# A GLU's last weight: all low parts on VectorE, a ring of six for the plain products' tokens, the first pair in another place

## The chip, the cores and the metric

The kernel runs on one core of a Trainium2 chip. The metric is the device time of one execution in microseconds; the time of a kernel is the median of its runs. TensorE multiplies, VectorE and ScalarE prepare its operands and take its results away, GpSimd (POOL) helps with elementwise work and issues the scatters of the output, SyncE (SP) issues nearly all transfers. Each engine works through its own instructions in order, and so does SP's queue of transfers.

## What is computed

Attention with a bias that decays with position, then a mixture of experts, then a gated linear unit. The change lies in the last of these. Cut to that part, the reference is:

```
def _moe2_ref(x, w_gate, w_val, w_out):           # x: 2304 tokens of 512; w_gate, w_val: 512 x 1536; w_out: 1536 x 512
    gate = 1.0 / (1.0 + np.exp(-(x @ w_gate)))
    val = x @ w_val
    return (gate * val @ w_out).astype(np.float32)
```

All numbers are float32.

## The kernel before

TensorE takes each float32 operand as two parts: a high part, which ScalarE makes by a cast to fp32r, and a low part, which is the operand minus its high part and comes from an elementwise subtraction. A product is then three matmuls: high by high, high by low, low by high.

The gated unit is class Moe2. Its first half makes h = gate * val for three blocks of 768 tokens (t = 0, 1, 2) and writes them to DRAM (`hd[t]`, shown as h). It runs as units (f, t, m) of seven slots; the last unit is n - 1, and two pieces of it, slot(n, 2) and slot(n, 4), run among the products that follow. The second half multiplies h by the last weight, w_out, and this is where the change lies. It has two stages.

**The plain products** (block 0). `final(q)`, q = 0 to 23, q = 12 g + f: for 384 tokens (group g) it adds the product of the f-th 128 rows of h with part f of the weight, nine matmuls of 512 columns (L1482 in the profile). It needs three things:

- part f of the weight, high and low. `load_o` brings twelve parts of 128 x 512 into four tiles `wr` (places a0_0 to a0_3 of the pool keep); `o_high(f)` casts on ScalarE (L1411), `o_low(f)` subtracts (L1417), on VectorE for f = 0 and 2, on GpSimd for the other ten.
- h of this f and g. `load_h(q)` (L1454) brings it into one of four tiles, the ring a1_4, a1_5, a1_0, a1_1. Load q + 4 stands in SP's queue behind `final(q)` and goes when that product has read the tile. `h_tasks(q)` then makes the high part on ScalarE (L1459) and the low part on VectorE (L1460); these stand two products ahead of `final(q)`.
- a PSUM accumulator for each of three rows of tokens. After f = 11 three copies (L1488, two on ScalarE and one on VectorE) and three scatters (L1464, GpSimd) take it away.

**The pair stage** (blocks 1 and 2). Six pairs j of 2 x 128 tokens each go through seven products by Strassen's scheme in Winograd's form (`p_slot(j, s)`, L1534). It needs sums of the weight's parts: `o_sums` makes eight sums in place in `wr` on VectorE (L1424) and from each of the four `wr` tiles a high part (`to`, ScalarE, L1439) and a low part (`to`, L1441: tiles 0 and 2 on VectorE, 1 and 3 on GpSimd). And it needs h of the pair: `load_p(j)` brings it in four transfers (tiles hp, L1501), and `p_tasks(j)` makes seven forms of it: casts on ScalarE (hf, L1261), low parts and sums on VectorE (hf, L1262, and hp, L1263). Before, `load_p(0)` goes into a1_2 and a1_6, and the loads of the other pairs take turns between a0_0 with a0_1 and a0_2 with a0_3, where `wr` was.

All this small work is placed by hand: a table `todo` says after which slot of the units a task is written, a table `later` after which product (its key is q). An engine sees its instructions in the order in which they are written. So what stands ahead of what on VectorE, ScalarE and SP follows from these tables, and within one key from the order of the `put` calls.

Of the kernel before, what the change touches and what calls it, by code (L numbers as in the profile page):

```python
# [8 lines left out]
F32 = mybir.dt.float32  # L9
F32R = mybir.dt.float32r  # L10
# [5 lines left out]
ALU = mybir.AluOpType  # L16
# [1185 lines left out]
class Moe2:  # L1202
# [210 lines left out]
        return high  # L1413

    def o_low(self, f):
        eng = self.nc.vector if f in (0, 2) else self.nc.gpsimd
        return lambda: eng.tensor_tensor(self.po[f][1], self.scr[f], self.po[f][0].bitcast(F32), ALU.subtract)  # L1417

    def o_sums(self):

        nc = self.nc
        W = [self.wr[i] for i in range(4)]
        lo, hi = slice(0, 256), slice(256, 512)
        sub = lambda o, x, y: lambda: nc.vector.tensor_tensor(o, x, y, ALU.subtract)  # L1424
        S = []
        for k in range(2):
            u, v = W[k], W[2 + k]
            S += [
                sub(u[:, :, lo], u[:, :, hi], u[:, :, lo]), sub(u[:, :, hi], v[:, :, hi], u[:, :, hi]),
                sub(v[:, :, hi], v[:, :, hi], u[:, :, lo]), sub(v[:, :, lo], v[:, :, lo], v[:, :, hi]),  # L1430
            ]
        self.to = {}

        def high(i, h):
            def f():
                tag = f"a2_{2 * i + h}" if 2 * i + h < 7 else "sg2"
                self.to[i, h] = self.ap.tile([128, 3, 512], F32R, tag=tag, name="to", bufs=1)
                if h == 0:
                    nc.scalar.copy(self.to[i, 0], W[i])  # L1439
                else:  # L1440
                    (nc.gpsimd if i % 2 else nc.vector).tensor_tensor(self.to[i, 1], W[i], self.to[i, 0].bitcast(F32), ALU.subtract)  # L1441

            return f

        return S, [high(i, h) for i in range(4) for h in range(2)]

    RING = (4, 5, 0, 1)

    def load_h(self, q):
        g, f = divmod(q, 12)
        t = self.hl[q] = self.ap.tile([128, 3, 512], F32R, tag=f"a1_{self.RING[q % 4]}", name="h0", bufs=1)[:, :, : self.G]
        self.nc.sync.dma_start(t[:, 2].bitcast(F32), self.hd[0][:, f, self.G * g : self.G * g + self.G])  # L1454

    def h_tasks(self, q):
# [36 lines left out]
    def load_p(self, j):  # L1493
        t, c0 = 1 + j // 3, 256 * (j % 3)
        raws = []
        for i in range(2):
            p, tag = (self.ap, f"a1_{(2, 6)[i]}") if j == 0 else (self.keep, f"a0_{2 * (j % 2) + i}")
            w = p.tile([128, 2, 6, 128], F32, tag=tag, name="hp", bufs=1)
            raws += [w[:, 0], w[:, 1]]
        for d, (i, h) in zip(raws, ((0, 0), (1, 1), (0, 1), (1, 0))):  # L1500
            self.nc.sync.dma_start(d, self.hd[t][:, 6 * h : 6 * h + 6, c0 + 128 * i : c0 + 128 * i + 128])  # L1501
        self.hr[j] = raws
# [86 lines left out]
    def run(self, ctx, rest):  # L1589

        NF, NT = self.NF, self.NT
        P = lambda c, n, **kw: c.enter_context(self.tc.tile_pool(name=n, bufs=1, reuse_waits="tile", **kw))
        self.ps, self.ap = P(ctx, "o_ps", space=PSUM), P(ctx, "o_a")
        self.units = [
            (f, t, m) for f in range(NF)
            for t, m in ([(0, 0), (0, 1), (1, 0), (2, 0), (1, 1), (2, 1)] if f == 0 else [(t, m) for m in range(2) for t in range(NT)])
        ]
        n = len(self.units)
        todo, self.late = {}, []

        def put(at, tasks):
            todo.setdefault(at, []).extend(tasks)

        def spread(first, last, tasks):
            for i, task in enumerate(tasks):
                put(first + (last - first + 1) * i // len(tasks), [task])

        at = lambda u, s: 7 * u + s
        for i, tasks in enumerate(rest):
            put(at(0, i), tasks)  # L1610
        raws = [[], [self.ap.tile([128, 2, self.G], F32, name=f"xs{i}", bufs=1) for i in range(3)]]
        raws[1].append(self.rp.tile([128, 1024], F32, tag="raw2_3", name="xs3", bufs=1)[:, : 2 * self.G].rearrange("p (c t) -> p c t", c=2))
        for i in range(2):
            w = self.ap.tile([128, 2, 2, self.G], F32, tag=f"a2_{5 + i}", name="xs", bufs=1)
            raws[0] += [w[:, 0], w[:, 1]]
        self.room_x(1, self.ap)
        for t in range(1, NT):
            self.load_x(t, raws[t - 1])
        spread(at(1, 0), at(2, 2), self.x_tasks(1, raws[0]))
        put(at(2, 2), [lambda: self.room_x(2, self.ap)])  # L1620
        spread(at(2, 3), at(3, 4), self.x_tasks(2, raws[1]))
        put(at(5, 0), [self.rows()])
        free = 0
        for f in range(1, NF):
            b = 6 * f - 6
            for m, soon, there in ((0, at(b + 1, 5), at(b + (4 if f == 1 else 3), 5)), (1, at(b + 4, 5), at(b + 6, 5))):
                soon = max(soon, free)
                blocks, parts = self.w_tasks(m)
                for stages, k in zip(blocks, (0, 1, 7, 8)):
                    for i, task in enumerate(stages):  # L1630
                        put(soon + k + i, [task])
                there = max(there, soon + 12)
                for i, tasks in enumerate(parts):
                    put(there + i, tasks)
                free = there + len(parts)
        put(at(n - 2, 5), [lambda: self.load_o(0)])
        put(at(n - 1, 0), [lambda: [(self.load_h(q), self.load_h(q + 1), self.load_o(1 + q // 2)) for q in (0, 2)]])
        put(at(n - 1, 1), [lambda: self.load_o(3)])
        oh, ol = [self.o_high(f) for f in range(12)], [self.o_low(f) for f in range(12)]
        for f in range(4):  # L1640
            put(at(n - 1, f + 1), [oh[f]])
            put(at(n - 1, f + 2), [ol[f]])
        for q in range(2):
            put(at(n - 1, 5 + q), self.h_tasks(q))
        for u in range(n):
            for s in range(7):
                now, self.late = self.late, []
                self.slot(u, s)
                for task in todo.pop(7 * u + s, []) + now:
                    task()  # L1650
        assert not todo
        later = {}

        def put(at, tasks):
            later.setdefault(at, []).extend(tasks)

        put(0, [lambda: self.slot(n, 2)])
        put(1, [lambda: self.slot(n, 4), lambda: [store() for store in self.late]])
        for q in range(2, 24):
            put(q - 2, self.h_tasks(q))  # L1660
        for f in range(4, 12):
            put((f - 4) // 2, [oh[f], ol[f]])
        sums, parts = [], []
        put(5, [lambda: [x.extend(y) for x, y in zip((sums, parts), self.o_sums())]])
        for i in range(8):
            put(6 + i, [lambda i=i: sums[i]()])
            put((10, 11, 14, 15, 11, 12, 15, 16)[i], [lambda i=i: parts[i]()])
        put(9, [lambda: self.load_p(0)])
        put(17, [lambda: self.load_p(1)])
        p = []  # L1670
        put(15, [lambda: p.extend(self.p_tasks(0))])
        cuts = (0, 2, 4, 6, 8, 11, 13, 15)
        for k in range(7):
            put(16 + k, [lambda i=i: p[i]() for i in range(cuts[k], cuts[k + 1])])
        for q in range(24):
            self.final(q)
            if q + 4 < 24:
                self.load_h(q + 4)
            for task in later.pop(q, []):
                task()  # L1680
        assert not later
        for j in range(self.NP + 1):
            for s in range(7):
                self.p_slot(j, s)
                if (j, s) == (0, 0):
                    for task in p[15:]:
                        task()
                if j + 1 < self.NP:
                    if s == 0:
                        x = self.p_tasks(j + 1)  # L1690
                    for task in x[(0, 0, 2, 5, 8, 11, 13)[s] : (0, 2, 5, 8, 11, 13, 18)[s]]:
                        task()
                if s == 6 and j + 2 < self.NP:
                    self.load_p(j + 2)
# [156 lines left out]
```

## Time and profile before

| | |
|---|---|
| runs shown | 988.88, 988.88, 997.13 us; median 988.88 |
| the profiled execution | 993.5 us, its span 991.7 us |
| TensorE busy over the span | 932.6 us (94%) |
| VectorE busy | 714.6 us (72%) |
| ScalarE busy | 557.3 us (56%) |
| GpSimd busy | 434.9 us (44%) |
| mean granted clock of TensorE | 0.981 of full speed |

Times of the trace are microseconds from the start of the span. Matmuls are pipelined: the duration shown for one includes its way through the array, so the rate is read from starts, or from a long unbroken piece of the chain of waits. PE is TensorE, DVE is VectorE, ACT is ScalarE, POOL is GpSimd, SP is SyncE; a q behind the name (SPq) means the engine's queue. In brackets behind an instruction stands the idle time before it and what ended it. The granted clock is given as a share of full speed; it has two levels, 1.2 and 2.4 GHz, so a mean between 0.5 and 1 is a mixture.

### The profile page before, as it was taken

Reading aid. Unit: us, or ns where it says so; the run is one execution under the profiler, and the core shown is the slowest. Engines: PE = TensorE matmul, PEld = TensorE weight load, DVE = VectorE, ACT = ScalarE, POOL = GpSimd, SP = SyncE. Lnnn points to the kernel's source line nnn. Section 1 sums busy time; section 2 is a strip of 40 time slices with the busy share of each in tenths; the row PEclk is TensorE's granted clock in tenths of the full one; section 3 lists DMA queues with packets and bytes.
Section 4 is the critical chain, followed back from the end, with each engine's and each line's share of the span. In section 5 each row is a group of like instructions: output and inputs, shape, how many; then the busy total and the mean of one; then the engine's idle time right before and its main releaser. Section 6 shows DMA issues by size and latency. Waiting matters only on the chain. (4 is left out here: it accounts for less than half of the span.)

```text
span 991.7 us, 18860 instructions
## 1 busy us (share of the span) xinstructions
PE 932.6 (94%) x6261; PEld 863.9 (87%) x6261; DVE 714.6 (72%) x1573; ACT 557.3 (56%) x1328; POOL 434.9 (44%) x639
## 2 busy tenths in 40 slices
PE   7999999999887999999999779999999999879996
PEld 6887888777676999999998769999999998659996
DVE  6889989998865678867635686776575747667771
ACT  5988888887623556666633454544445344434431
POOL 7877787896863577876540000100000006222111
PEclk8999999999998999999999989999999999999999
DMA  6655448794674145922357522332332307553411
GB/s 165 156 128 137 111 91 96 175 111 71 213 67 59 59 150 160 329 87 86 117 164 262 150 67 85 96 107 95 108 122 84 113 25 265 181 167 106 148 57 43
DMA packets 164578, 124.32 MB, mean 125 GB/s; under 512 B 86897, under 2 KB 146828, under 8 KB 164470
## 3 DMA queue, kind: packets, MB, share of 16 engines
q1 hardware_dynamic: 159462, 112.57, 43.6%
q0 software_dynamic: 3792, 10.14, 3.1%
q8 instruction: 52, 0.85, 0.4%
q14 instruction: 56, 0.46, 0.2%
q10 hardware_dynamic: 1216, 0.30, 0.1%
HBM read 115.95 MB, written 32.18 MB: 149 GB/s over the span
## 5 line engine op out<-in xcount | busy, mean ns | idle before, releaser
L1326 PE MATMUL X<-a,set 128*128 128x384 f32 x864 | 166.6, 341 | 7.6 <-ACT u L1335 4.3
L1326 PEld LDWEIGHTS X<-a,set 128*128 128x128 f32 x864 | 154.1, 192 | 9.6 <-ACT u L1335 4.9
L845 POOL TENSOR_SCALAR dn<-dr 128x256 int8<-128x256 int8 (+1 forms) x60 | 33.7, 562 | 262.6 <-DMA dr<-in_moe_w_gate_dram 118.1
L170 POOL TENSOR_SCALAR bias<-cumB,cumT 128x576 f32<-128x576 f32 (+4 forms) x155 | 82.5, 534 | 41.8 <-DVE nm L289 30.9
L909 POOL TENSOR_TENSOR w<-raw,w 128x512 fp32r<-128x512 f32 x56 | 79.3, 1427 | 41.4 <-ACT w L906 38.5
L973 PE MATMUL ph<-xT,w 128*128 128x256 f32 x672 | 92.0, 287 | 1.9 <-DVE w L909 1.9
L298 ACT ACTIVATE P<-P,nm 64x64 f32<-64x64 f32 (+4 forms) x160 | 89.6, 563 | 2.7 <-DVE nm L289 2.6
L973 PEld LDWEIGHTS ph<-xT,w 128*128 128x128 f32 x672 | 85.4, 194 | 2.1 <-DVE w L909 2.1
L289 DVE CUSTOM_DVE_ANT_0 P<-sb,bias 128x576 f32<-128x576 f32 (+4 forms) x160 | 72.0, 479 | 17.9 <-PE sb L280 14.6
L1326 PE MATMUL Y<-a,set 128*128 128x384 f32 x432 | 81.1, 335 | 0.0
L339 DVE TENSOR_TENSOR PL<-pt,PH 128x512 fp32r<-128x512 f32 (+3 forms) x160 | 78.8, 530 | 2.7 <-ACT PH L331 1.7
L1326 PEld LDWEIGHTS Y<-a,set 128*128 128x128 f32 x432 | 75.8, 188 | 0.1
L331 ACT CAST PH<-pt 128x512 fp32r<-128x512 f32 (+3 forms) x160 | 67.0, 466 | 9.8 <-PE pt L317 7.1
L317 PE MATMUL pt<-ident,P 128*128 128x128 f32 (+2 forms) x480 | 69.2, 274 | 1.4 <-DVE PL L339 0.8
L977 ACT ACTIVATE hH<-ph 128x256 fp32r<-128x256 f32 x72 | 27.7, 385 | 75.2 <-PE ph L973 65.3
L1464 POOL DMA_INDIRECT out_dram<-oy,row x18 | 20.9, 1163 | 108.0 <-ACT oy L1549 56.2
L909 DVE TENSOR_TENSOR w<-raw,w 128x512 fp32r<-128x512 f32 x56 | 59.9, 1071 | 11.1 <-ACT w L906 10.3
L1335 ACT COPY u<-X 128x384 f32<-128x384 f32 x72 | 34.5, 479 | 59.1 <-PE X L1326 59.0
L317 PEld LDWEIGHTS pt<-ident,P 128*128 128x128 f32 (+2 forms) x480 | 52.6, 130 | 13.1 <-issue 6.6
L906 ACT CAST w<-raw 128x512 fp32r<-128x512 f32 x112 | 63.5, 619 | 0.0
L362 PE MATMUL ot<-PH,vhl 128*128 128x512 f32 (+4 forms) x160 | 62.0, 398 | 0.0
L280 PE MATMUL sb<-KT,QH 128*128 128x288 f32 (+3 forms) x192 | 56.2, 317 | 4.1 <-DVE nm L289 3.3
(299 smaller groups left out, 2424.5 us busy)
## 6 DMA issues: line engine op xcount, KB each, us to landing
raw<-in_moe_w_dram SPq DMA_DIRECT2D x80, 512.0 KB
h<-sg SPq DMA_DIRECT2D x72, 192.0 KB
cumB<-cum_d SPq DMA_DIRECT2D x32, 288.0 KB
hp<-h SPq DMA_DIRECT2D x24, 384.0 KB
qraw<-in_q_dram SPq DMA_DIRECT2D x58, 128.0 KB
dr<-in_moe_w_out_dram SPq DMA_DIRECT2D x12, 511.6 KB
dr<-in_moe_w_gate_dram SPq DMA_DIRECT2D x24, 255.2 KB
dr<-in_moe_w_val_dram SPq DMA_DIRECT2D x24, 255.2 KB
```

Source lines behind the costliest of these rows:

```text
L170: (nc.vector if n in FILLB else nc.gpsimd).tensor_scalar(res[i][:rows], cumB[:rows, :m], -1.0, self.cumT[:rows, i, n : n + 1], ALU.mult, A ...
L280: nc.tensor.matmul(self.sb[:rows, o : o + c1 - c0], X[:, T0[i] : T0[i] + rows], h["KT"][:, c0:c1], start=j == 0, stop=j == 1)
L289: nc.vector.tensor_tensor_reduce(out=pt[:rows], in0=self.sb[:rows, o : o + m], in1=self.bias_t[n][i][:rows], op0=ALU.add, op1=ALU.min, sca ...
L298: nc.scalar.activation(h["P"][i][:rows], h["P"][i][:rows], AF.Exp, bias=h["nm", i][:rows], scale=-1.0, accum_out=self.sums_t[(n // 2) % 3] ...
L317: nc.tensor.transpose(pt[: TS[j], c : c + TS[i]], h["P"][i][: TS[i], T0[j] : T0[j] + TS[j]], self.ident[: TS[i], : TS[i]])
L331: nc.scalar.copy(t[:r, a:z], pt[:r, a:z])
L339: nc.vector.tensor_tensor(t[:r, a:z], pt[:r, a:z], h["H"][u][:r, a:z].bitcast(F32), ALU.subtract)
L362: nc.tensor.matmul(out[:, q0 : q0 + z - a], w, X[: TS[j], a:z], start=k == 0, stop=k == len(mm) - 1, skip_group_check=True)
L906: nc.scalar.copy(v, src)
L909: (eng or nc.vector).tensor_tensor(v, src, h.bitcast(F32), ALU.subtract)
L973: nc.tensor.matmul(ph, w[:, 128 * dc : 128 * dc + 128], x[:, dc], start=k == 0, stop=k == 11)
L1326: self.nc.tensor.matmul(bank, w[:, c], a[:, h, c], start=first and k == 0, stop=k == 5, skip_group_check=True)
```

## The change

`o_low` subtracts all twelve parts on VectorE, and so does the low part of every `to`. The ring has six tiles, a1_4, a1_5, a1_0, a1_1, a1_2, a1_6, with loads 4 and 5 written among the slots of the last unit. Since a1_2 and a1_6 now belong to the ring, the first pair goes to a0_0 and a0_1, the place of the first two `wr` tiles, and the keys of the sums, the `to` parts, the pairs' loads and the first pair's tasks move.

```
     def o_low(self, f):
-        eng = self.nc.vector if f in (0, 2) else self.nc.gpsimd
-        return lambda: eng.tensor_tensor(self.po[f][1], self.scr[f], self.po[f][0].bitcast(F32), ALU.subtract)
+        return lambda: self.nc.vector.tensor_tensor(self.po[f][1], self.scr[f], self.po[f][0].bitcast(F32), ALU.subtract)
...
                 else:
-                    (nc.gpsimd if i % 2 else nc.vector).tensor_tensor(self.to[i, 1], W[i], self.to[i, 0].bitcast(F32), ALU.subtract)
+                    nc.vector.tensor_tensor(self.to[i, 1], W[i], self.to[i, 0].bitcast(F32), ALU.subtract)
...
-    RING = (4, 5, 0, 1)
+    RING = (4, 5, 0, 1, 2, 6)
...
-        t = self.hl[q] = self.ap.tile([128, 3, 512], F32R, tag=f"a1_{self.RING[q % 4]}", name="h0", bufs=1)[:, :, : self.G]
+        t = self.hl[q] = self.ap.tile([128, 3, 512], F32R, tag=f"a1_{self.RING[q % 6]}", name="h0", bufs=1)[:, :, : self.G]
...
-            p, tag = (self.ap, f"a1_{(2, 6)[i]}") if j == 0 else (self.keep, f"a0_{2 * (j % 2) + i}")
-            w = p.tile([128, 2, 6, 128], F32, tag=tag, name="hp", bufs=1)
+            w = self.keep.tile([128, 2, 6, 128], F32, tag=f"a0_{2 * (j % 2) + i}", name="hp", bufs=1)
...
+        for q in (4, 5):
+            put(at(n - 1, 2 * q - 5), [lambda q=q: self.load_h(q)])
...
-        put(5, [lambda: [x.extend(y) for x, y in zip((sums, parts), self.o_sums())]])
+        put(3, [lambda: [x.extend(y) for x, y in zip((sums, parts), self.o_sums())]])
         for i in range(8):
-            put(6 + i, [lambda i=i: sums[i]()])
-            put((10, 11, 14, 15, 11, 12, 15, 16)[i], [lambda i=i: parts[i]()])
-        put(9, [lambda: self.load_p(0)])
-        put(17, [lambda: self.load_p(1)])
+            put((4, 5, 6, 7, 8, 8, 9, 10)[i], [lambda i=i: sums[i]()])
+            put((8, 9, 11, 12, 9, 13, 12, 14)[i], [lambda i=i: parts[i]()])
+        put(12, [lambda: self.load_p(0)])
+        put(15, [lambda: self.load_p(1)])
         p = []
-        put(15, [lambda: p.extend(self.p_tasks(0))])
-        cuts = (0, 2, 4, 6, 8, 11, 13, 15)
+        put(13, [lambda: p.extend(self.p_tasks(0))])
+        cuts = (0, 2, 4, 6, 8, 9, 11, 13, 15, 18)
...
-            if q + 4 < 24:
-                self.load_h(q + 4)
+            if q + 6 < 24:
+                self.load_h(q + 6)
...
-                if (j, s) == (0, 0):
-                    for task in p[15:]:
-                        task()
```

What the change moves is seen in the order of instructions on three engines. Line numbers behind the edits fall by one to three (L1482 becomes L1481, L1460 becomes L1459, L1417 becomes L1416, L1441 becomes L1440). Numbers in names are tiles in the order in which they were made.

VectorE at the first products. h_14605, h_14607, h_14613 and h_14615 are h of products 0 to 3 and h_14703, h_14729 of products 4 and 5. Before, from the last low part that VectorE has:

```order
L1417 TENSOR_TENSOR set<-wr,set 128x512
L1460 TENSOR_TENSOR h_14605<-h_14605 128x384
L1354 TENSOR_TENSOR u_14685<-Y,u_14685 128x384
L1356 TENSOR_TENSOR sg<-u_14685,sg 128x384
L1460 TENSOR_TENSOR h_14607<-h_14607 128x384
L1356 TENSOR_TENSOR sg<-X,sg 128x384
L1460 TENSOR_TENSOR h_14613<-h_14613 128x384
L1354 TENSOR_TENSOR u_14652<-Y,u_14652 128x384
L1356 TENSOR_TENSOR sg<-u_14652,sg 128x384
L1460 TENSOR_TENSOR h_14615<-h_14615 128x384
L1460 TENSOR_TENSOR h_14703<-h_14703 128x384
L1460 TENSOR_TENSOR h_14729<-h_14729 128x384
```

and now, from the same place on, where h_14654 and h_14677 are h of products 4 and 5:

```order
L1459 TENSOR_TENSOR h_14613<-h_14613 128x384
L1416 TENSOR_TENSOR wo<-wr,wo 128x512 x2
L1354 TENSOR_TENSOR u_14652<-Y,u_14652 128x384
L1356 TENSOR_TENSOR sg<-u_14652,sg 128x384
L1459 TENSOR_TENSOR h_14615<-h_14615 128x384
L1416 TENSOR_TENSOR set<-wr,set 128x512 x2
L1459 TENSOR_TENSOR h_14654<-h_14654 128x384
L1416 TENSOR_TENSOR set<-wr,set 128x512 x2
L1459 TENSOR_TENSOR h_14677<-h_14677 128x384
L1416 TENSOR_TENSOR wo<-wr,wo 128x512 x2
```

Eight low parts of the weight now stand in pairs between h of products 2 and 6.

VectorE around the first pair's first low part (`hf`). h_14839, h_14853, h_14870, h_14888 and h_14917 are h of products 13 to 17. Now:

```order
L1487 COPY oy<-acc 128x512
L1459 TENSOR_TENSOR h_14839<-h_14839 128x384
L1459 TENSOR_TENSOR h_14853<-h_14853 128x384
L1440 TENSOR_TENSOR to<-wr,to 128x1536
L1459 TENSOR_TENSOR h_14870<-h_14870 128x384
L1440 TENSOR_TENSOR to<-wr,to 128x1536
L1459 TENSOR_TENSOR h_14888<-h_14888 128x384
L1440 TENSOR_TENSOR to<-wr,to 128x1536
L1262 TENSOR_TENSOR hf<-hp,hf 128x768
L1459 TENSOR_TENSOR h_14917<-h_14917 128x384
```

Before, two of these three `to` were GpSimd's, the sums of `wr` were spread over the same products, and `hf` stood behind h of product 18. Now three `to` and `hf` stand ahead of h of products 15, 16 and 17.

SP's queue around the pairs' loads. Before, h_14861 is the load of product 13 and h_15013 that of product 21:

```order
L1454 DMA h_14861<-h_65 128x384
L1501 DMA hp<-h_66 128x6x128 x4
L1454 DMA h_14881<-h_65 128x384
L1454 DMA h_14912<-h_65 128x384
L1454 DMA h_14933<-h_65 128x384
L1454 DMA h_14949<-h_65 128x384
L1454 DMA h_14963<-h_65 128x384
L1454 DMA h_14978<-h_65 128x384
L1454 DMA h_14995<-h_65 128x384
L1454 DMA h_15013<-h_65 128x384
L1501 DMA hp<-h_66 128x6x128 x4
L1454 DMA h_15036<-h_65 128x384
```

and now, where h_14935 is the load of product 18 and h_15014 that of product 22:

```order
L1453 DMA h_14935<-h_65 128x384
L1499 DMA hp<-h_66 128x6x128 x4
L1453 DMA h_14958<-h_65 128x384
L1453 DMA h_14973<-h_65 128x384
L1453 DMA h_14991<-h_65 128x384
L1499 DMA hp<-h_66 128x6x128 x4
L1453 DMA h_15014<-h_65 128x384
L1453 DMA h_15029<-h_65 128x384
```

The first pair's four transfers move from behind the load of product 13 to behind that of product 18, and the second pair's follow them three loads later.

## Rows read from the trace of the kernel before

**Rows 1.** Windows: length, busy PE, PEld, DVE, ACT, POOL (instructions), clock, DMA share, GB/s.

```profile
820.00:893.00 73.00, 63.33 (x274) 50.55 (x273) 53.28 (x59) 31.67 (x54) 27.14 (x16) 0.98 0.63 201
893.00:985.00 92.00, 90.59 (x755) 90.18 (x753) 58.57 (x76) 36.31 (x61) 15.41 (x15) 1.00 0.28 93
...
860.00:871.00 11.00, 5.87 (x23) 3.82 (x22) 8.84 (x8) 4.08 (x6) 4.13 (x2) 1.00 0.43 154
871.00:877.00 6.00, 6.00 (x20) 4.71 (x19) 4.98 (x5) 4.23 (x7) 3.49 (x1) 0.72 0.11 33
```

**Rows 2.** Groups by line, 820 to 895: count | busy, mean ns | idle before, releasers.

```profile
L1482 PE MATMUL acc<-set,h 128*128 128x512 f32 x126 | 30.5, 393 | 3.2 <-ACT h L1459 2.2 <-DVE h L1460 1.0
L1482 PE MATMUL acc<-wo,h 128*128 128x512 f32 x90 | 24.7, 423 | 6.4 <-DVE h L1460 3.5 <-ACT h L1459 3.0
...
L1460 DVE TENSOR_TENSOR h<-h 128x384 fp32r<-128x384 f32 x24 | 21.5, 911 | 14.0 <-ACT h L1459 13.8
```

**Rows 3.** Timeline of TensorE: start, length, instructions, idle before and its releaser.

```profile
827.18 0.63 PE L1482 MATMUL acc<-set,h 128*128 128x512 f32 x2
828.80 1.88 PE L1482 MATMUL acc<-set,h 128*128 128x512 f32 x7 [1.00 <-DVE h L1460]
...
837.71 6.09 PE L1482 MATMUL acc<-wo,h 128*128 128x512 f32 x25 [0.27 <-DVE h L1460]
...
855.97 4.28 PE L1482 MATMUL acc<-set,h 128*128 128x512 f32 x18
862.48 2.48 PE L1482 MATMUL acc<-set,h 128*128 128x512 f32 x9 [2.23 <-ACT h L1459]
...
866.07 2.37 PE L1482 MATMUL acc<-wo,h 128*128 128x512 f32 x9 [0.65 <-DVE h L1460]
870.70 5.54 PE L1482 MATMUL acc<-wo,h 128*128 128x512 f32 x16 [2.25 <-DVE h L1460]
...
887.06 2.48 PE L1482 MATMUL acc<-wo,h 128*128 128x512 f32 x9 [2.62 <-ACT h L1459]
...
892.66 1.24 PE L1534 MATMUL X<-set,hf 128*128 128x256 f32 x9
```

**Rows 4.** The chain of waits that ended last: start, length, what.

```profile
830.71 3.63 DMA h<-h
...
837.71 17.52 PE acc L1482 x76
855.24 6.60 DMA h<-h
...
879.67 6.73 DMA h<-h
```

**Rows 5.** Timeline of VectorE, a sum of wr .

```profile
865.94 4.24 DVE L1424 TENSOR_TENSOR wr<-wr 128x768 f32<-128x768 f32 x1
```

**Rows 6.** Timeline of GpSimd at the same place.

```profile
865.51 3.85 POOL L1441 TENSOR_TENSOR to<-wr,to 128x1536 fp32r<-128x1536 f32 x1 [5.24 <-ACT to L1439]
```

**Rows 7.** Tiles wr and h: count, shortest/median/longest ns, first and last start.

```profile
L1424 DVE TENSOR_TENSOR wr<-wr x8: 949/952/4239, 845.7 to 865.9; 128x768 f32<-128x768 f32 x8
...
L1417 DVE TENSOR_TENSOR set<-wr,set x2: 674/1229/1784, 824.8 to 826.5; 128x512 fp32r<-128x512 f32 x2
L1441 DVE TENSOR_TENSOR to<-wr,to x2: 1751/1752/1752, 857.7 to 862.9; 128x1536 fp32r<-128x1536 f32 x2
...
L1460 DVE TENSOR_TENSOR h<-h x24: 543/558/3532, 828.2 to 890.3; 128x384 fp32r<-128x384 f32 x24
```

**Rows 8.** Timeline of ScalarE behind product 11.

```profile
856.17 0.59 ACT L1488 COPY oy<-acc 128x512 f32<-128x512 f32 x1 [0.81 <-PE acc L1482]
856.65 0.52 ACT L1459 CAST h<-h 128x384 fp32r<-128x384 f32 x1
857.06 1.48 ACT L1439 CAST to<-wr 128x1536 fp32r<-128x1536 f32 x1
```

**Rows 9.** Timeline of SP's queue: the first pair's four transfers.

```profile
852.39 2.73 SPq L1501 DMA_DIRECT2D hp<-h  x4
```

More of the change, by code (lines that the diff above doesn't have):

```diff
@@ L1663, in run @@
         sums, parts = [], []
-        put(5, [lambda: [x.extend(y) for x, y in zip((sums, parts), self.o_sums())]])
+        put(3, [lambda: [x.extend(y) for x, y in zip((sums, parts), self.o_sums())]])
         for i in range(8):
-            put(6 + i, [lambda i=i: sums[i]()])
-            put((10, 11, 14, 15, 11, 12, 15, 16)[i], [lambda i=i: parts[i]()])
-        put(9, [lambda: self.load_p(0)])
-        put(17, [lambda: self.load_p(1)])
+            put((4, 5, 6, 7, 8, 8, 9, 10)[i], [lambda i=i: sums[i]()])
+            put((8, 9, 11, 12, 9, 13, 12, 14)[i], [lambda i=i: parts[i]()])
+        put(12, [lambda: self.load_p(0)])
+        put(15, [lambda: self.load_p(1)])
         p = []
-        put(15, [lambda: p.extend(self.p_tasks(0))])
-        cuts = (0, 2, 4, 6, 8, 11, 13, 15)
-        for k in range(7):
-            put(16 + k, [lambda i=i: p[i]() for i in range(cuts[k], cuts[k + 1])])
+        put(13, [lambda: p.extend(self.p_tasks(0))])
+        cuts = (0, 2, 4, 6, 8, 9, 11, 13, 15, 18)
+        for k in range(9):
+            put(14 + k, [lambda k=k: [task() for task in p[cuts[k] : cuts[k + 1]]]])
         for q in range(24):
             self.final(q)
-            if q + 4 < 24:
-                self.load_h(q + 4)
+            if q + 6 < 24:
+                self.load_h(q + 6)
             for task in later.pop(q, []):
```

## The prediction

> **What bounds the kernel now.** I read the windows first [rows 1]. From 820 to 893 us TensorE is busy 63.3 of 73 us; in the pair stage behind it, 893 to 985, it is busy 90.6 of 92. So only the plain products (L1482, product q = 0 to 23) have time to give back, and what is removed there moves the end: the pair stage hangs on TensorE alone, and starts when the products end. The grouped lines say how much is plain idleness: 3.2 + 6.4 = 9.6 us before L1482, behind VectorE's h (L1460) or ScalarE's h (L1459) [rows 2]. TensorE's timeline says where [rows 3]: 1.00 us before the third matmul of product 0, 2.23 before product 14, 2.25 inside product 16, 2.62 before product 22, 0.27 in product 3 and 0.65 in product 15; the sum leaves 0.6 more, around product 23. The chain of waits names what was late [rows 4]: for product 14 a load of h, 6.60 us from issue to landing, for product 22 another of 6.73; for product 16 nothing but VectorE.
>
> The stage lasts from 827.18 to 892.66, 65.5 us [rows 3]. 76 matmuls without a gap take 17.52 us, 0.2305 each [rows 4]; 216 of them are 49.8 us. Twelve matmuls of 384 columns are left over from the stage before (slot(n, 2) and slot(n, 4)); by columns 0.173 each, 2.1 in all, an estimate. So 51.9 us are work and 13.6 are lost: 9.6 idle, 1.7 because the clock granted from 871 to 877 was 0.72 on average, part of it at the lower of its two levels (1.2 instead of 2.4 GHz), after a stretch of 11 us in which TensorE had worked 5.9 (6 x 0.28 [rows 1]), and some 2.3 of restarts after eight gaps. **13.6 us is the most that this change can give.**
>
> **The change, part by part.**
>
> *VectorE instead of GpSimd.* Ten low parts of 512 columns (all but parts 0 and 2) and two of 1536 (L1441) move. Alone on VectorE they take 0.674 and 1.752 us [rows 7]: 6.7 + 3.5 = 10.2 us more for VectorE. What VectorE gets back: its h subtraction takes 0.558 us at the median, but 24 of them were busy 21.5 us [rows 2, 7], 8.1 too many; of the wr sums one took 4.239 instead of 0.952, 3.3 too many; of its own two low parts one took 1.784 instead of 0.674, 1.1 too many. That is 12.5 us, so VectorE's busy time falls by some 2 us although it gets more work. That GpSimd stretches these is in the timelines: the sum of 4.24 us begins at 865.94 [rows 5], and GpSimd's subtraction runs from 865.51 to 869.36 [rows 6]; h of product 16 stands behind it and TensorE waits until 870.70. No GpSimd subtraction is left, so this 2.25 goes, the 0.27 of product 3 (its h stood in the same way), the 0.65 of product 15, and the low clock behind them.
>
> The Trainium skill speaks to this on two pages. "Perfetto Trace Analysis", section Optimizing Scalar/DVE Operations, says that a saturated VectorE may be relieved by giving work to ScalarE or GpSimd, though the shared port may spoil it; by that alone the change would go the wrong way, and the sum would be rival B's. "SBUF — State Buffer", section Who interferes with whom, says that a VectorE instruction with two SBUF inputs and a GpSimd instruction that reads SBUF lock each other out for a whole instruction; by that all 12.5 us go, and the sum is the one below. The 4.24 us row, which ends after GpSimd's does, agrees with the second page.
>
> *Product 0.* Its low h is waited for 1.00 us. In front of it VectorE has one low part that falls from 1.78 to 0.67, and now one more (part 3) of 0.67: 0.44 earlier. I leave 0.55 of this gap.
>
> *Parts 4 to 11.* They stand on VectorE in pairs ahead of h3, h4, h5 and h6: 2 x 0.67 + 0.56 = 1.9 us for each product of 9 x 0.2305 = 2.07 us. This fits, by little. The high half of part 9 must wait for slot(n, 4), which still reads the tile it overwrites, and h5 stands behind that on ScalarE; slot(n, 4) runs three products earlier than product 5. No gap.
>
> *The ring of six.* Load q is issued when product q - 6 ends instead of q - 4: five products (10.4 us) to land in instead of three (6.2). The undisturbed load behind product 0 took 3.63 us, the two behind a pair's transfers 6.60 and 6.73 [rows 4]; with 0.5 for ScalarE's cast and 0.56 for VectorE's h that is 7.8, over 6.2 and under 10.4. So the gaps of 2.23 and 2.62 go, and the 0.6 behind the second. Loads 4 and 5 now lie in tiles that the stage before has left, and no longer wait for product 0 (830.71 [rows 4]).
>
> *The first pair elsewhere.* Its four transfers go into the place of the weight's raw parts 0 and 1 and can begin only when these are subtracted; this is the one new wait. Let T be the end of product 11, 855.97 in the trace of before [rows 3]. ScalarE after T, in its order: output copy until T + 0.8, h13, `to` (1.48), h14 until T + 3.0, `to`, h15 until 4.8, h16 until 5.2 [rows 8]. VectorE: h14 until 3.6, `to` of part (1,1) until 5.3, h15 5.7, `to` 7.4, h16 7.9, `to` 9.5, the pair's first low part (768 columns, 0.95 like a sum of wr [rows 7]) 10.4, h17 10.9. TensorE needs h17's low at T + 5 x 2.07 + 2 x 0.23 = 10.8. It comes within 0.1 us: this is the tightest place of the whole stage, h15 and h16 have 0.8 or more. On SP the pair's third transfer holds the queue until T + 5.3; load 19 stands behind it, goes at about T + 6.5 instead of 4.1, and is wanted at T + 16.6. Even 6.7 us of landing and 1.1 of conversion leave 2.
>
> *The pair's tasks* now end with product 22 and not inside the pair stage. Of the operations none is new, and their tiles come free two products earlier. The order inside the pair stage stays. I cost this at nothing; the cover is the 90.6 of 92 us.
>
> **Sum.** 13.6 lost, minus 0.55 that stays at product 0, minus 0.35 for the near miss at h17 and one restart: 12.7 us gained. The profiled execution took 993.5 us (span 991.7 and 1.8 around it): 980.8. The median of the runs, 988.88, is 4.6 below that execution; the same gain there gives **976.2 us**.
>
> **Rivals.**
>
> *A, the pair's first transfer is late for VectorE.* Its first low part stands ahead of h17. Before, the four transfers began at 852.39 and the load behind them landed at 861.84 [rows 4, 9], so 9.4 us bounds the landing of the first. Issued at T + 2.1, it would land at 11.5; with cast (0.83 by the sizes of the casts in [rows 8], an estimate), low part and h17 that is 13.9 against 10.8, a gap of 3.1, and if the clock falls again 1.7 more. Gain 8 to 9.6: 979.3 to 980.9. For it: in-order VectorE. Against it: only a quarter of the data stands in front, which at an equal share is 2.4 us.
>
> *B, the other side: VectorE becomes the bound.* If the stretched operations were slowed by something that stays (transfers, ScalarE), VectorE would keep its 12.5 us and get 10.2 more, ahead of h3 to h6 and h15 to h17, where TensorE waits. With the ring's 5.5 us gained it is 4.7 us slower, 993.6; with the ring worth nothing 10.2 slower, 999.1. It decides when more than 2.07 us of VectorE stand in front of each h. Against it: VectorE has 53.3 of 73 us [rows 1], and both `to` that ran on it alone took 1.75 to the hundredth [rows 7].
>
> *C, the ring buys nothing at the second pair.* SP is in order, and the second pair waits for `to` (3,1), T + 9.5; if VectorE runs 3 us late, loads 22 and 23 land as late as now, and 2.62 + 0.6 stay. Gain 9.5: 979.4.
>
> *D, only half is done:* the gaps go but loads of the burst (both pairs and six loads, 4.3 MB, from T + 2 on) delay one another so that several gaps of a us come up. Gain 5 to 8: 981 to 984.
>
> **How the numbers follow.** Forecast 0.62, A 0.14, B 0.06, C 0.07, D 0.11. The forecast's own range is 972 to 980: a gain of 11.5 to 13.6, and the executions of before, which lie 4 us and more apart on their own (988.88, 993.5, 997.13). The range reaches down to 972 and up to 985, over A, C and D. A difference of 1% (9.9 us) is about what a measurement of this kernel can tell from none. Faster by over 1% needs under 979: nearly all of the forecast and a share of A and C, 0.64. Slower by over 1% is the end of B, 0.03. Within 1% is the rest, 0.33.
>
> **What would show it.** Right: VectorE's h all at 0.56 us, no gap of TensorE over 0.6 between product 0 and the pair stage, clock 1.00 throughout, the first L1532 matmul about 53 us after the first of L1481. A: a gap at product 17 behind VectorE's h, whose predecessor waited for the pair's cast. B: VectorE without idleness between products 3 and 7, or 12 and 17, and stretched h. C and D: ScalarE's h waiting for a load after product 18. The prediction is wrong if the stage keeps more than 57 us, or if the pair stage opens gaps that it did not have.

## The result, and the profile after

The changed kernel took 980.15 us (median of 4 runs, 977.86 to 984.64), the kernel before, on the same chip, 989.88 us (988.88 to 997.13). The ratio is 0.9878 with a 95% interval of 0.9841 to 0.9914: about 12 us less. The two medians by themselves are 9.7 us apart, a ratio of 0.990. The profiled execution took 984.64 us, its span is 982.9.

TensorE in the stage of the plain products, from its timeline (start, length, instructions, idle time before and its releaser; these answer to [rows 3]):

```profile
830.47 0.73 PE L1481 MATMUL acc<-set,h 128*128 128x512 f32 x2
831.39 1.89 PE L1481 MATMUL acc<-set,h 128*128 128x512 f32 x7 [0.18 <-DVE h L1459]
...
858.04 6.32 PE L1481 MATMUL acc<-set,h 128*128 128x512 f32 x27
864.20 6.65 PE L1481 MATMUL acc<-wo,h 128*128 128x512 f32 x27
...
883.01 1.24 PE L1532 MATMUL X<-set,hf 128*128 128x256 f32 x9
```

From 830.47 to 883.01 the stage takes 52.5 us, where it took 65.5 [rows 3]. One gap of 0.18 us is left in product 0, and nothing else is listed: 9.6 us of idleness [rows 2] have become 0.2. Products 15 to 17 (864.20) take 6.65 us; with VectorE's chain ahead of h17 one step shorter they take 6.46 (e9_tail_late, below). That is the near miss at h17, 0.2 us.

The windows of the same trace (length, busy PE, PEld, DVE, ACT, POOL with instructions, granted clock, DMA share, GB/s), the stage before, the plain products, and the pair stage:

```profile
820.00:830.47 10.47, 10.47 (x61) 10.24 (x60) 6.94 (x13) 4.52 (x9) 0.00 (x0) 1.00 0.91 294
830.47:883.01 52.54, 52.36 (x229) 42.62 (x229) 44.03 (x63) 27.97 (x46) 3.42 (x4) 1.00 0.65 210
883.01:975.00 91.99, 91.19 (x757) 90.57 (x755) 56.29 (x74) 35.72 (x60) 15.65 (x14) 1.00 0.32 104
```

The clock is 1.00 throughout the stage, so the dip to 0.72 [rows 1] went with the gaps. VectorE has 44.0 of 52.5 us, 84%, and holds TensorE up by no more than these 0.4 us.

VectorE's instructions on the tiles h and wr (count, shortest/median/longest ns, first and last start; these answer to [rows 7]):

```profile
L1459 DVE TENSOR_TENSOR h<-h x24: 547/551/562, 830.8 to 878.4; 128x384 fp32r<-128x384 f32 x24
...
L1423 DVE TENSOR_TENSOR wr<-wr x8: 948/950/959, 844.1 to 854.8; 128x768 f32<-128x768 f32 x8
L1416 DVE TENSOR_TENSOR set<-wr,set x7: 681/684/685, 827.0 to 841.3; 128x512 fp32r<-128x512 f32 x7
...
L1440 DVE TENSOR_TENSOR to<-wr,to x4: 1751/1752/1753, 851.8 to 865.8; 128x1536 fp32r<-128x1536 f32 x4
```

The longest h is 0.562 us, it was 3.532; the longest sum is 0.959, it was 4.239. Nothing stretches any more.

The stage gave 12.9 us, the profiled execution only 8.9 (993.5 to 984.6). The difference lies on both sides of the stage. It began at 830.47 instead of 827.18, 3.3 us late, in code that the change does not touch: in the window from 300 to 320 us, for one, the granted clock was 0.67 and not 0.83 as in the trace of before. In the traces of the kernels below the stage begins anywhere between 825.6 and 833.5. And the rest of the span behind the stage took 99.9 us instead of 99.0. That part has a new wait, and it is shown below. To compare kernels I therefore use, beside the times, the length of the stage, from the first L1481 (L1482 in the kernel before) to the first L1532 (its line number is 1533 or 1534 in some), and the rest from there to the end of the span.

### The profile page after: what moved, and what is told of

It is laid out like the page before. It is cut to its first block, busy times and chain, and to the rows that moved or that the text cites. A ratio compares the mean times of both kernels' runs of the same rounds, so it can differ in the third digit from the quotient of the medians.

```text
span 982.9 us, 18850 instructions
## 1 busy us (share of the span) xinstructions
PE 929.4 (95%) x6261; PEld 864.6 (88%) x6261; DVE 710.5 (72%) x1585; ACT 556.6 (57%) x1328; POOL 410.2 (42%) x627
## 5 line engine op out<-in xcount | busy, mean ns | idle before, releaser
L1463 POOL DMA_INDIRECT out_dram<-oy,row x18 | 20.0, 1113 | 168.3 <-ACT oy L1487 90.6
L317 PEld LDWEIGHTS pt<-ident,P 128*128 128x128 f32 (+2 forms) x480 | 52.8, 130 | 10.5 <-issue 5.9
```

What stands on the lines that cost most here:

```text
L317: nc.tensor.transpose(pt[: TS[j], c : c + TS[i]], h["P"][i][: TS[i], T0[j] : T0[j] + TS[j]], self.ident[: TS[i], : TS[i]])
```

## The experiments

### Two halves

What each half does by itself. First the changed kernel with GpSimd's share given back (e1_pool_back):

```
     def o_low(self, f):
-        return lambda: self.nc.vector.tensor_tensor(self.po[f][1], ...)
+        eng = self.nc.vector if f in (0, 2) else self.nc.gpsimd
+        return lambda: eng.tensor_tensor(self.po[f][1], ...)
...
-                    nc.vector.tensor_tensor(self.to[i, 1], ...)
+                    (nc.gpsimd if i % 2 else nc.vector).tensor_tensor(self.to[i, 1], ...)
```

> The changed kernel, but ten low parts of the weight and two of the to parts are GpSimd's again, as before; the ring of six and the new places stay. By the lock theory (a VectorE instruction with two SBUF inputs waits out a GpSimd instruction that reads SBUF): VectorE's h and wr subtractions stretch again to 1.6 to 4 us wherever GpSimd subtracts, a gap of about 1 us returns in product 0 and one of 2 to 4 us around products 15 to 17, where VectorE's chain had no slack; the stage from the first plain product to the pair stage takes 56 to 59 us instead of 52.5 and the time is 3.5 to 7 us above the changed kernel's. By rival B (the stretching came from transfers or ScalarE, not from GpSimd): the stage stays within 0.5 us of 52.5. If the ring alone is what matters: the same, 52.5 to 53.

Measured: ratio to before 0.9954 (0.9929 to 0.9979), stage 62.7 us. TensorE's gaps, from its timeline, and VectorE's and GpSimd's timelines at the largest of them:

```profile
845.00 6.11 PE L1482 MATMUL acc<-wo,h 128*128 128x512 f32 x25 [1.18 <-DVE h L1460]
...
873.99 3.35 PE L1482 MATMUL acc<-set,h 128*128 128x512 f32 x7 [5.98 <-DVE h L1460]
```

```profile
866.30 8.11 DVE L1460 TENSOR_TENSOR h<-h 128x384 fp32r<-128x384 f32 x2 [1.23 <-ACT h L1459]
```

```profile
866.66 6.85 POOL L1441 TENSOR_TENSOR to<-wr,to 128x1536 fp32r<-128x1536 f32 x2
```

Two h subtractions, 1.1 us of work, take 8.11 us: GpSimd subtracts from 866.66 to 873.51, VectorE's second h ends just after, and TensorE waits 5.98 us for it. The lock theory holds, and by more than expected (56 to 59): the new keys put the two `to` of GpSimd directly behind one another, and the gap lies inside product 14 and not at products 15 to 17. In the window around its end, 870 to 878, the clock was 0.58 on average. Rival B expected 52.5 and is out.

Then the kernel before with that edit alone, the ring and the order untouched (e3_dve_only):

> The kernel before with one edit: all low parts on VectorE; ring of four, order and places as before. By the lock theory: h on VectorE at 0.56 us throughout, the gaps of 0.27, 0.65 and 2.25 us and the low clock behind them are gone, the gaps of 2.23, 2.62 and 0.6 before products 14, 22 and 23 stay; the stage takes 59 to 60.5 us instead of 65.5 and the time is 5 to 6.5 us under that of before. By rival B (VectorE gets 10.2 us of work and nothing back): 65 to 70 us, no faster or slower.

Measured: ratio 0.9954 (0.9921 to 0.9987), stage 62.1 us instead of the 59 to 60.5 expected. All 24 h are at 0.547 to 0.559 us, so the first step worked. But:

```profile
867.25 3.91 PE L1481 MATMUL acc<-set,h 128*128 128x512 f32 x9 [3.82 <-ACT h L1458]
...
887.81 6.00 PE L1481 MATMUL acc<-wo,h 128*128 128x512 f32 x18 [2.16 <-ACT h L1458]
```

and, in the chain of waits of the same kernel:

```profile
838.60 19.96 PE acc L1481 x87
858.56 8.05 DMA h<-h
```

TensorE now comes to product 14 sooner, and its load lands later, 8.05 us after its issue instead of 6.60 [rows 4]. The gap there grows from 2.23 to 3.82. Behind this gap and behind the next one matmuls run at the clock's lower level for a while (nine take 3.91 us, otherwise 2.24; the windows 865 to 872 and 887 to 894 have a clock of 0.76 each), which cost 1.7 us twice. So much of the time that VectorE got back was spent waiting for the load.

One half gave 2.8 us of the stage (e1), the other 3.4 (e3), both together 12.9. The halves do not add up.

### The ring, by its size

The changed kernel with a ring of four or five tiles (the tail of the first pair's tasks one product later in both, since their tiles come free later), for four (e2_ring_four):

```
-    RING = (4, 5, 0, 1, 2, 6)
+    RING = (4, 5, 0, 1)
...
-        for q in (4, 5):
-            put(at(n - 1, 2 * q - 5), [lambda q=q: self.load_h(q)])
...
-        cuts = (0, 2, 4, 6, 8, 9, 11, 13, 15, 18)
+        cuts = (0, 2, 4, 6, 8, 9, 9, 11, 13, 15)
...
-            if q + 6 < 24:
-                self.load_h(q + 6)
+            if q + 4 < 24:
+                self.load_h(q + 4)
...
+                if (j, s) == (0, 0):
+                    for task in p[15:]:
+                        task()
```

> The changed kernel with a ring of four tiles again (a1_4, a1_5, a1_0, a1_1), loads four ahead, and the last of the first pair's tasks one product later, since their tiles come free later; all low parts on VectorE, pairs in the new places. By the theory that the ring carries 2.23 + 2.62 + 0.6 us of the gain: gaps before the products whose loads stand behind a pair's transfers (17 or 18, and 20 to 22), each 0.8 to 4 us, behind ScalarE's h that waits for a load; the stage takes 55 to 58 us instead of 52.5, the time is 2.5 to 5.5 us above the changed kernel's. By the rival that the ring is not needed once VectorE runs freely: 52.5 to 53.5 and no wait of ScalarE for a load that TensorE feels.

> The changed kernel with a ring of five tiles (a1_4, a1_5, a1_0, a1_1, a1_2), loads five ahead, and the tail of the first pair's tasks as with the ring of four. A load then has four products, 8.3 us; the slow loads need 6.7 to land, 1.1 to be converted, and up to 1 us more where SP holds them behind the pair's third transfer. Theory: one gap at most, under 1.5 us, around product 18 or 21; stage 52.5 to 54 us. By the rival that only the order and places matter and not the lead: the same as with four tiles.

Measured with four: ratio 0.9901 (0.9862 to 0.9941), stage 54.9 us, just under the 55 to 58 expected. With five: 0.9866 (0.9806 to 0.9926), stage 53.0. With four, TensorE has one gap that counts:

```profile
868.68 2.49 PE L1481 MATMUL acc<-wo,h 128*128 128x512 f32 x9 [1.82 <-ACT h L1458]
```

It is product 17, whose load stands behind the first pair's transfers. The second pair, which I had expected to give a gap too, gives none. So in the new order two tiles more are worth 2.3 us (54.9 to 52.5), of which the first brings 1.9. The sixth is worth 0.5 us, less than the times can tell. A ring of six with the old order was not run, so what the ring is worth there is not known.

### The place and the key of the first pair

From e3_dve_only (62.1) to e2_ring_four (54.9) the ring is the same and VectorE does all subtractions in both. What differs is the order: the sums and `to` earlier, the pairs' loads behind products 12 and 15 instead of 9 and 17, the first pair's tasks earlier, and its place. The place alone is tested by putting the first pair back (e8_ring_four_pair_apart):

```
-            w = self.keep.tile([128, 2, 6, 128], F32, tag=f"a0_{2 * (j % 2) + i}", name="hp", bufs=1)
+            p, tag = (self.ap, f"a1_{(2, 6)[i]}") if j == 0 else (self.keep, f"a0_{2 * (j % 2) + i}")
+            w = p.tile([128, 2, 6, 128], F32, tag=tag, name="hp", bufs=1)
```

> The ring of four with the changed kernel's order (e2_ring_four, stage 54.9 us), but the first pair's transfers go to a1_2 and a1_6 again, as before: nothing holds them, all four go at once behind the load of product 16. If the place matters (in a0_0 and a0_1 the third and fourth wait for a low part, so a load of h meets only half of the pair's data): the load of product 17 stands behind all four, lands 6.6 to 8 us after its issue, the gap before product 17 grows from 1.8 to 3 or 4 us, and the stage takes 56 to 58.5 us. If only the keys matter (the pair's loads later, the sums earlier): 54.5 to 55.5 us, gap 1.5 to 2.

Measured: ratio 0.9924 (0.9899 to 0.995), stage 55.5 us, the gap before product 17 is 2.44 us and not 1.82. That lies at the edge of what the keys alone would give and under what the place would: the new place, whose third transfer waits for a subtraction, is worth 0.6 us by itself (one trace of each) and is otherwise there to make room for the ring.

Then one key alone, in e3_dve_only (e11_dve_pair_later):

```
-        put(9, [lambda: self.load_p(0)])
+        put(12, [lambda: self.load_p(0)])
```

> The kernel before with all low parts on VectorE (e3_dve_only, stage 62.1 us) and one key more: the first pair's transfers stand behind the load of product 16 instead of 13, so that they no longer run beside the three scatters of product 11 (0.8 MB). If the scatters made the load behind the pair late (8.05 us of landing in e3_dve_only, 5.6 in e8_ring_four_pair_apart): the load of product 17 lands in under 6 us, its gap is 1.8 to 2.6 us instead of 3.8, and the clock may stay up; the gap before product 22 (2.2 us) and the low clock behind it stay; stage 58.5 to 60.5 us. If it is the ring of four alone: the gap only moves to product 17 and stays 3.5 to 4 us, stage 61.5 to 62.5.

Measured: ratio 0.9946 (0.9923 to 0.997), stage 59.7 us, 2.4 less than e3_dve_only. The gap of 3.82 is replaced by one of 1.67 before product 17 and two of 0.65 behind VectorE's h. The gap of 2.16 before product 22, which was to stay, is 1.27, and the windows 866 to 873 and 884 to 891 have a clock of 1.00:

```profile
861.05 4.00 PE L1481 MATMUL acc<-wo,h 128*128 128x512 f32 x16 [0.65 <-DVE h L1459]
866.71 2.49 PE L1481 MATMUL acc<-wo,h 128*128 128x512 f32 x9 [1.67 <-ACT h L1458]
869.04 2.75 PE L1481 MATMUL acc<-set,h 128*128 128x512 f32 x11
872.44 5.97 PE L1481 MATMUL acc<-set,h 128*128 128x512 f32 x25 [0.65 <-DVE h L1459]
879.68 2.48 PE L1481 MATMUL acc<-wo,h 128*128 128x512 f32 x9 [1.27 <-ACT h L1458]
```

So where the pair stands matters. But the 2.4 us are not the gap alone: TensorE's idle time over the stage falls only from 6.4 to 5.3 us (1.1 us), while the low clock, which cost twice 1.7 us in e3_dve_only, is gone; by what is left over, restarts behind more gaps take part of that back. And the explanation by the scatters is not borne out. By it the load of product 17 was to land in under 6 us. It is issued at 859.46, and ScalarE waits for it until 866.15, 6.7 us later:

```profile
859.46 10.10 SPq L1453 DMA_DIRECT2D h<-h  x5
```

```profile
866.15 0.51 ACT L1458 CAST h<-h 128x384 fp32r<-128x384 f32 x1 [5.39 <-DMA h<-h]
```

Nor did the scatters lie otherwise in the kernel before. The first of the three scatters of product 11 (128 x 512 numbers each, 0.8 MB in all), in e3_dve_only and then in the kernel before:

```profile
858.82 1.10 POOL L1463 DMA_INDIRECT out_dram<-oy,row  x1 [69.53 <-ACT oy L1487]
```

```profile
855.64 1.11 POOL L1464 DMA_INDIRECT out_dram<-oy,row  x1 [13.70 <-ACT oy L1488]
```

In e3_dve_only it starts 0.3 us behind the issue of the load of product 14 (858.56), which lands 8.05 us after its issue; before, 0.4 us behind it (855.24 [rows 4]), and that load lands after 6.60. Why the load of e3_dve_only took 8.05 us, and why the clock fell there and not in e11_dve_pair_later, stays open. What the remaining 4.2 us between e11_dve_pair_later and e8_ring_four_pair_apart consist of was not taken apart key by key; the gaps above name them: `to` and sums between h of products 14 to 19, and the second pair's load behind the load of product 21.

### What of GpSimd's work holds VectorE

The changed kernel with useless work on GpSimd, gated by a small copy on ScalarE, behind products 4, 6, 8 and 10: a subtraction of 1536 columns that reads and writes a spare tile (e5_pool_reads), or three fillings of that tile, which only write (e6_pool_writes).

```
+            self.nc.scalar.copy(t, d[:, 0:1])
+            self.nc.gpsimd.tensor_tensor(d, d, d, ALU.subtract)       # e5
...
+            for _ in range(3):                                        # e6
+                self.nc.gpsimd.memset(d, 0.0)
```

> The changed kernel with four useless subtractions of 1536 columns in place added on GpSimd, which read and write a spare tile, one each behind products 4, 6, 8 and 10, each gated by a small copy on ScalarE; nothing else differs. By the lock theory each takes 3.5 to 3.9 us and holds the VectorE instruction with two SBUF inputs that meets it: h and wr on VectorE show four instructions or more of 2 to 4 us between products 4 and 12, and TensorE gets gaps of one to some us there, because VectorE has little slack. By rival B (GpSimd beside VectorE does not matter): all h at 0.55 and all wr at 0.95 us, and no gap.

> Like e5_pool_reads, but each of the four places on GpSimd has three fillings of the spare tile (about 1.4 us each, nothing read) instead of a subtraction. If what holds VectorE is GpSimd's reading: all h at 0.55 and wr at 0.95 us on VectorE although GpSimd is busy beside them some 4 us at a time, no gap over 0.6 us, stage 52.3 to 53. If any GpSimd work does it: stretched instructions and gaps as in e5_pool_reads (stage 59.2).

Each of the two kernels ran once, so their traces are compared and not their times. Measured with the subtractions: stage 59.2 us, 6.6 more, with four gaps of 0.65 to 1.92 us. Four of VectorE's instructions take 3.1 to 3.4 us. Two of them beside GpSimd, e5_pool_reads (the second is the first of the pair that takes 3.86):

```profile
841.59 3.10 DVE L1459 TENSOR_TENSOR h<-h 128x384 fp32r<-128x384 f32 x1
844.61 3.86 DVE L1416 TENSOR_TENSOR set<-wr,set 128x512 fp32r<-128x512 f32 x2
```

```profile
841.37 2.91 POOL L1678 TENSOR_TENSOR spare<-spare 128x1536 f32<-128x1536 f32 x1 [16.41 <-ACT gate L1677]
844.58 2.75 POOL L1678 TENSOR_TENSOR spare<-spare 128x1536 f32<-128x1536 f32 x1 [0.30 <-ACT gate L1677]
```

With the fillings, e6_pool_writes, where GpSimd was busy for 4.27 us at a time:

```profile
838.82 4.28 POOL L1679 MEMSET spare<- 128x1536 f32 x3 [16.15 <-ACT gate L1677]
843.38 4.27 POOL L1679 MEMSET spare<- 128x1536 f32 x3 [0.28 <-ACT gate L1677]
```

```profile
L1459 DVE TENSOR_TENSOR h<-h x24: 546/550/559, 829.8 to 877.5; 128x384 fp32r<-128x384 f32 x24
```

No VectorE instruction is stretched and the stage takes 52.8 us. It is GpSimd's subtraction, which reads, that holds VectorE's subtractions, each for about the length of GpSimd's instruction, and not GpSimd's being busy or writing. The Trainium skill, "SBUF — State Buffer", section Who interferes with whom, says both halves of this; the two runs agree with it.

### The wait that came up in the pair stage

In the changed kernel VectorE waits at the head of the pair stage for a scatter of the second group to have read its tile. VectorE, SP's queue and GpSimd there:

```profile
888.74 0.42 DVE L1545 TENSOR_TENSOR oy<-Z,p 128x256 f32<-128x256 f32 x1 [5.49 <-DMA out_dram<-oy,row]
```

```profile
880.77 49.72 SPq L1499 DMA_DIRECT2D hp<-h  x16
```

```profile
882.67 0.97 POOL L1463 DMA_INDIRECT out_dram<-oy,row  x1 [21.27 <-ACT oy L1487]
```

The first pair's tasks end earlier, so its place comes free earlier, and SP sends the third pair's transfers at 880.77, 1.9 us ahead of the first scatter. Before, VectorE had no wait at that instruction. I took the order of these two for the cause. To test it, two keys moved (e9_tail_late): the pair's first low part one product later, and its last three tasks behind p_slot(0, 0), as they were before the change.

```
-        cuts = (0, 2, 4, 6, 8, 9, 11, 13, 15, 18)
+        cuts = (0, 1, 4, 6, 8, 9, 9, 11, 13, 15)
...
                 self.p_slot(j, s)
+                if (j, s) == (0, 0):
+                    for task in p[15:]:
+                        task()
```

> The changed kernel with two keys moved: the first pair's first low part stands one product later on VectorE (behind h of product 17), and the pair's last three tasks are written behind p_slot(0, 0), as before, so that SP gets the place of the third pair's transfers some 3 us later, after the scatters of the second group are on their way. Theory: the stage loses its 0.2 us at product 17 (52.3 instead of 52.5), VectorE no longer waits 5.5 us for a scatter in the pair stage, and that stage is 0.3 to 0.6 us shorter; in all 0.5 to 0.8 us under the changed kernel, which the times can hardly tell but the two stretches of the profile can. Rival: the third pair's loads have nothing to do with the scatters' 5.9 us; then VectorE's wait of 5 us or more stays.

> The changed kernel once more, to see on one chip and beside the others how far its stretches repeat: stage of the plain products 52.5 us within 0.3, VectorE's wait of 5.5 us for a scatter in the pair stage again, time 1.0 to 1.5% under that of before.

Measured: e9_tail_late 980.16 us, ratio 0.9863 (0.9835 to 0.989); e10_same, the changed kernel again on the same chip, 983.49 us, ratio 0.9901 (0.9874 to 0.9929). The intervals overlap, so the times do not tell them apart. The profiles do: stage 52.4 against 52.6 us, the extra 0.2 at products 15 to 17 gone (6.46 for 27 matmuls), and VectorE's wait gone. VectorE and the first scatter in e9_tail_late:

```profile
883.06 0.96 DVE L1262 TENSOR_TENSOR hf<-hp,hf 128x768 fp32r<-128x768 f32 x1 [2.42 <-ACT hf L1261]
884.07 0.42 DVE L1545 TENSOR_TENSOR oy<-Z,p 128x256 f32<-128x256 f32 x1
```

```profile
879.24 0.97 POOL L1463 DMA_INDIRECT out_dram<-oy,row  x1 [21.09 <-ACT oy L1487]
```

Here SP sent the third pair at 880.70, 1.5 us behind the first scatter. But the edit moved VectorE too. With the pair's last tasks ahead of it, it comes to this instruction 4.8 us after the first scatter started; in the changed kernel it stood idle from 883.25 on (888.74 less 5.49), 0.6 us after the first scatter, and went on 6.1 us after it, in e10_same 5.2 us after it. So some 4.2 of the 5.49 us are VectorE coming sooner, and at most 1.3 the scatter landing later. The kernel before says the same:

```profile
897.16 0.42 DVE L1547 TENSOR_TENSOR oy<-Z,p 128x256 f32<-128x256 f32 x1
```

```profile
892.32 1.16 POOL L1464 DMA_INDIRECT out_dram<-oy,row  x1 [17.07 <-ACT oy L1488]
```

There too VectorE came 4.8 us after the first scatter and had no wait, although SP had sent the third pair at 883.40, 8.9 us ahead of it.

In e10_same the wait was 4.33 us and TensorE did not feel it; in the first profile of the changed kernel TensorE lost 0.22 us to it. In e6_pool_writes TensorE lost 1.34 at the same place, behind a wait of 6.58 us of VectorE for which the profile names a matmul and not the scatter. I had expected 0.3 to 0.6 us from its removal; against e10_same it is 0.05 in the rest of the span (99.42 against 99.47), against the first profile 0.5 (99.89). So the wait is real and comes mainly from the pair's last tasks, which no longer stand ahead of that instruction; that the third pair's transfers make the scatter later is not shown. What it costs TensorE varies from nothing to some 1.3 us.

## Why the prediction was right, and which of its terms were not

**The bound and the place.** The time was in the plain products, and what was removed there moved the end. This held: the stage 52.5 us (52.6 in e10_same) where the sum gave 52.8, a gain of 12.9 for 12.7. The ratio that the prediction implied, 976.2 to 988.88, is 0.987; 0.9878 was measured, and 0.9901 when the same kernel ran again (e10_same). The median itself, 980.15, came out some 4 us above 976.2, just over the forecast's own range (972 to 980) and among the times given to rival A. The time alone therefore did not pick the forecast; the trace did. Runs of the same kernel differ by several microseconds (977.86 to 984.64), and the profiled run lost 3.3 us in front of the stage.

**VectorE instead of GpSimd.** The mechanism is shown, by e1, e3, e5 and e6. One gap was put down to it wrongly: h of product 15 began on VectorE at 865.47, ahead of GpSimd's subtraction (865.51 [rows 6]), and took 0.55 us. It was late because h of product 14 had waited for its load and a `to` and a sum stood between the two, so its 0.65 us came from the load. Parts of 512 columns cost 0.684 us (0.674 assumed), `to` 1.752 as assumed. VectorE at 84% of the stage is faster than VectorE relieved by GpSimd (52.5 against 62.7 us, e1). That the relief may be spoilt by the shared port is what the Trainium skill, "Perfetto Trace Analysis", section Optimizing Scalar/DVE Operations, adds to its advice; here it was.

**Product 0.** 0.55 us were to stay. 0.18 stayed in the profile of the changed kernel, 0.37 in e10_same.

**The chain behind product 11.** With T = 858.04, h17 was to end at T + 10.9; it ended at 868.90, T + 10.86, and cost the 0.2 us that the near miss was given. The first pair's cast began 7.6 us after T (865.68) and so left the chain alone; rival A did not come about.

**The ring.** This is the step that was mis-sized. The prediction put the gaps before products 14, 22 and 23, 5.4 us, down to the ring of four, and 3.2 us of gaps and the clock to GpSimd. In the new order the ring of six is worth 2.3 us over four (e2), and VectorE instead of GpSimd 10.2 (62.7 to 52.5, e1). In the old order VectorE's share is worth 3.4 (e3). Taken one after the other, VectorE, then the order, then the ring, the shares are 3.4, 7.2 and 2.3; by another way they are others. The sum came out right because every cause was removed; the shares did not, because I read each gap of before as belonging to one cause. A gap hides what stands behind it: with GpSimd out of the way TensorE only came earlier to a load that was no sooner there (3.82 instead of 2.23 us), and its clock fell.

**The first pair elsewhere.** Costed at nothing beside the near miss. Its place and key did more than that: the key alone took 2.4 us off (e3 to e11), and the whole new order 7.2 (e3 to e2). The change in order was treated as making room for the ring; along that way it was the largest single part. Of these 7.2 us 3.4 are the clock, which fell twice in e3 and stays at 1.00 in e2.

**The pair's tasks.** "I cost this at nothing": nearly so, but the cover named, TensorE's 90.6 of 92 us, is itself what waits there. With the tasks ended earlier VectorE comes to its first output of the pair stage some 4 us sooner and waits there for a scatter, and TensorE lost 0.2 us to it in one profile and nothing in the next. By its letter this is one of the prediction's own signs of being wrong, a gap that the pair stage did not have; at 0.22 us it changes nothing in the sum.

**Rivals.** B is out by e6 (GpSimd busy, nothing stretched) and by e5. C, loads 22 and 23 late: ScalarE waited for no load after product 18 that TensorE felt. D: no gaps of a microsecond came up.

## What to carry to other kernels

Before GpSimd is given a subtraction that reads SBUF beside a busy VectorE, look in the timeline for VectorE instructions far longer than their median and for what GpSimd ran just then. Here a subtraction that would have cost VectorE 1.75 us held it up for 3.3 and TensorE for 2.25. When several waits lie on one path, one gap after another, do not add their lengths per cause: measure the length of the whole stage, and be ready for the next gap to grow when one cause alone is removed, as it did here from 2.23 to 3.82 us. When a burst of large transfers stands in an in-order queue ahead of small ones that are wanted soon, try where it stands as well as more buffers: here one key took 2.4 us off, and in the new order two more tiles another 2.3.

## What was not expected of the hardware

A gap of TensorE does not tell by its length whether the granted clock falls behind it. In e3_dve_only it fell behind gaps of 3.82 and 2.16 us (0.76 over the 7 us around each), and before the change behind the gap of 2.25 (0.72 from 871 to 877). Before the change a gap of 2.62 us was followed by 1.00 (884 to 893 us), and in e8_ring_four_pair_apart one of 2.44 by nine matmuls at the full rate, 2.49 us. The price where it fell was 1.7 us in each of these three places, on top of the gap.
